# Retention and a softplus feed-forward net on one core: attention in groups of two steps, every fourth slot

## The chip, the cores and the metric

The kernel runs on one core of a Trainium2 chip. The metric is the device time of one execution, in microseconds (us). The engines are named as in the profile: PE is the matrix engine, PEld its loading of weights, DVE, ACT and POOL the vector, scalar and general engines, SP the queue that issues the transfers.

## The reference

Eight sequences of 576 tokens, eight heads of 64 features. Attention is a retention: scores decay with distance, there is no softmax. Its output, 4608 tokens by 512 features, goes through a two-layer net with a softplus between.

```python
def _attn_ref(q, k, v):                      # (8, 8, 576, 64) each
    scores = matmul(q, k.T) / sqrt(64)
    gamma = 1.0 - 2.0 ** (-5.0 - arange(8))  # one per head
    Dmat = where(rel >= 0, gamma ** rel, 0.0)  # rel = query position - key position
    return matmul(scores * Dmat, v)

def _moe_ref(x, w_in, w_out):                # x (4608, 512), w_in (512, 2048), w_out (2048, 512)
    h = x @ w_in
    g = maximum(h, 0.0) + log1p(exp(-abs(h)))
    return g @ w_out
```

## The kernel before

**The net.** The 4608 tokens are cut into 9 units of 512. A unit goes through 16 slots, one for each 128 of the 2048 hidden features, so there are 144 slots (`for i in range(NSLOT)`). A slot has these parts. On PE, `hidden_mm(i)` makes h for 128 features and 512 tokens from 12 products of 128x128 weights with 512 columns: 4 blocks of input features times 3 terms, since each 32-bit number is split into a high and a low part. ACT then takes the absolute value of h, the exponential and the logarithm (`logs`, L270 to L272); DVE adds max(h, 0) (`softplus`, L276, which reads h from PSUM); ACT rounds the result to the high part of g (L280), and DVE subtracts for the low part (`softplus_rest`, L284). Last on PE comes `output_mm(i - 1)`: the slot before's g times w_out, again 12 products, which add to four banks y over the 16 slots of the unit. So PE's order in each slot is hidden products of this slot, output products of the slot before. After a unit's last output products ACT and DVE copy two banks y each to SBUF (L304, L306) and SP sends them off.

**PSUM.** There are eight banks: four hold y, two hold h in turn (`ps_h`, two buffers, so that h of one slot can be written while h of the slot before is still read), and two hold one attention tile, `bank` (`ps_att`, one buffer of two banks).

**Attention.** The tokens are also cut into 36 chunks of 128, and heads into four pairs; a step is one chunk and two pairs (four heads), so there are 72 steps, two for each chunk. Nine steps are done in an opening ahead of the slots. After that each odd slot begins with one visit of PE to attention, for step m, 9 + (i - 1) / 2, until slot 127. A visit has four products of 64x64 blocks, each product 8 such matmuls (the profile has two records for each, 16 in all): the scores of step m (`scores`, L156), its sums of keys times values for the running state (`sums`, L169), and, for step m - 1, the masked scores times values (`values`, L220) and the state times queries (`cross`, the second loop of `values`, L231). Sequences begin at the start or in the middle of a chunk; some steps there have half of their sums or of their L231 matmuls only.

A 64x64 matmul takes one quadrant of PE's array: a row group (which 64 partitions of SBUF it reads) and a column group (which 64 partitions of PSUM it writes). In the text a quadrant is called a lane. `t` is the half of the chunk, `h` the head of the pair; the scores read row group h and write column group t, the other products read row group t and write column group h. All products of row group 0 go to the first of the two banks of `bank`, all of row group 1 to the second. The columns of a bank are divided into scores, sums and values.

**What follows a visit.** DVE multiplies the values by the decay (`values_out`, x, L241), ACT and POOL split x into its high and low parts for the net (L246, L247); DVE masks the scores (`scores_out`, a, L178) and adds up the state (`states_out`: u, sx and s, L201, L202, L210, or copies at a sequence's start); POOL copies half of sx and decays s (L194, L212). Then SP loads step m + 1 (`load_step`, one transfer of 576 KB into one of two buffers `rawp`), and POOL scales its values (L145). Results of step m's visit are used at the next visit, two slots later.

**What sets the order.** The order on each engine is the order in which the program writes its instructions; nothing is scheduled anew. Until about slot 15 the slots also turn the weights into their high and low parts as they arrive (`weight_...`), on ACT and DVE.

Of the kernel before, what the change touches and what calls it, by code (L numbers as in the profile page):

```python
# [33 lines left out]
KQ, RAW = 2 * C + 2 * QC, 6 * C + 2 * QC  # L34
SCOLS, TCOLS, VCOLS = slice(0, C), slice(C, 2 * C), slice(2 * C, 3 * C)
# [5 lines left out]
NOPEN = AHEAD + 2  # L41
FIRST_HALF = NF // 2
# [18 lines left out]
def retention_softplus_ffn(ctx: ExitStack, tc, first, others, consts, w, out):  # L61
# [56 lines left out]
    def load_step(m):  # L118

        if m == 0:  # L120
            at = 0
            for x in parts:
                nc.sync.dma_start(x, first[:, at:at + x.shape[1]])
                at += x.shape[1]
            kq, kv = parts[0][:, 0:KQ], parts[1][:, 0:4 * C]
# [23 lines left out]

    def scores(m, bank):  # L150
        if m >= NSTEP:
            return
        L = live[m]
        for s in range(2):
            for t, h in quads:
                nc.tensor.matmul(bank[rows[t], h, SCOLS][:, part[s]], L["k"][rows[h], s, part[t]],  # L156
                                 L["q"][rows[h], s, part[t]], start=True, stop=True, skip_group_check=True)
        L["bank"] = bank

    def sums(m):  # L160

        if m >= NSTEP:
            return
        L = live[m]
        start, follows = _chunk_kind(m // 2)
        for s in range(2):
            for t, h in quads:
                if follows if t else start != HC:
                    nc.tensor.matmul(L["bank"][rows[h], t, TCOLS][:, part[s]], L["kp"][rows[t], s, rows[h]],  # L169
                                     L["v"][rows[t], s, rows[h]], start=True, stop=True, skip_group_check=True)  # L170

    def scores_out(m):

        if m >= NSTEP:
# [4 lines left out]
                             L["bank"][:, :, SCOLS].rearrange("p h (s c) -> p h s c", s=2),  # L179
# [3 lines left out]
    def states_out(m):  # L183
# [6 lines left out]
        sum0, sum1 = (L["bank"][:, t, TCOLS].rearrange("p (s d) -> p s d", s=2) for t in range(2))  # L190
# [23 lines left out]

    def values(m, bank):

        L = live[m]
        for s in range(2):
            for t, h in quads:
                nc.tensor.matmul(bank[rows[h], t, VCOLS][:, part[s]], L["v"][rows[t], s, rows[h]],  # L220
                                 L["a"][rows[t], h, s], start=(s == 0), stop=L["states"][t] is None,
                                 skip_group_check=True)
        for s in range(2):
            for t, h in quads:
                if L["states"][t] is None:
                    continue
                if t == h:
                    lhs, rhs = L["states"][t], L["q"][rows[t], s, part[t]]
                else:
                    lhs, rhs = L["sx"], L["q"][rows[t], s, C:QC]  # L230
                nc.tensor.matmul(bank[rows[h], t, VCOLS][:, part[s]], lhs[rows[t], s], rhs, start=False, stop=True,  # L231
                                 skip_group_check=True)

    def values_out(m, bank, rest):

        live.pop(m)
# [5 lines left out]
                             bank[:, :, VCOLS].rearrange("p t (s c) -> p s t c", s=2),  # L242
# [11 lines left out]
    def hidden_mm(i, cols=slice(0, T)):  # L254
# [3 lines left out]
        h = ps_h.tile([P, T], F32, tag="h", name="h")[:, cols]  # L258
# [277 lines left out]
```

## Time and profile before

| | |
|---|---|
| time, median of 3 runs | 906.99 us (904.97 to 908.05) |
| time of the profiled execution | 907.14 us |
| its span, first to last instruction | 905.4 us |
| granted TensorE clock | 0.994 |
| busy in the span: PE, PEld | 889.3 us, 724.9 us |
| busy in the span: DVE, ACT, POOL | 366.4 us, 443.3 us, 144.9 us |
| transfers | 70.37 MB, mean 78 GB/s |

The span leaves 1.74 us of the profiled execution's time outside. A time in the trace counts from the start of the span. The row of a group gives the line of the kernel, the engine, the operation, the tile written and the tiles read, the shapes, the number of records, the busy time and the mean of one record, and behind the second bar the idle time ahead of it on its engine with what ended it. In the chain of waits each piece is a start, a length, and the engine, tile and line that the time is put down to; consecutive records of a line are merged. In the timeline a merged row gives the start, the time from the first record's start to the last one's end, and what was idle before.

### The profile page before, as it was taken

Reading aid. Unit: us, or ns where it says so; the run is one execution under the profiler, and the core shown is the slowest. Engines: PE = TensorE matmul, PEld = TensorE weight load, DVE = VectorE, ACT = ScalarE, POOL = GpSimd, SP = SyncE. Lnnn points to the kernel's source line nnn. Section 1 sums busy time; section 2 is a strip of 40 time slices with the busy share of each in tenths; the row PEclk is TensorE's granted clock in tenths of the full one; section 3 lists DMA queues with packets and bytes.
Section 4 is the critical chain, followed back from the end, with each engine's and each line's share of the span. In section 5 each row is a group of like instructions: output and inputs, shape, how many; then the busy total and the mean of one; then the engine's idle time right before and its main releaser. Section 6 shows DMA issues by size and latency. Waiting matters only on the chain.

```text
span 905.4 us, 18152 instructions
## 1 busy us (share of the span) xinstructions
PE 889.3 (98%) x7826; PEld 724.9 (80%) x7826; DVE 366.4 (40%) x742; ACT 443.3 (49%) x771; POOL 144.9 (16%) x269
## 2 busy tenths in 40 slices
PE   6899999999999999999999999999999999999998
PEld 5677778888888888888888888888888888888886
DVE  5788963333332343333333333323332432332222
ACT  5687764344444444444444444444444444445444
POOL 3312211111111111111111111111111111100000
PEclk9899999999999999999999999999999999999999
DMA  9565623111211131111211131113111121101001
GB/s 362 185 206 199 211 81 100 53 54 54 98 33 49 54 100 54 54 52 38 90 54 53 54 100 53 30 51 101 53 54 54 64 67 50 54 1 47 1 1 46
DMA packets 20527, 70.37 MB, mean 78 GB/s; under 512 B 2272, under 2 KB 2272, under 8 KB 20448
## 3 DMA queue, kind: packets, MB, share of 16 engines
q1 hardware_dynamic: 20448, 69.23, 22.9%
q8 instruction: 61, 1.00, 0.5%
q14 instruction: 18, 0.15, 0.0%
HBM read 59.78 MB, written 9.44 MB: 76 GB/s over the span
## 4 chain that ended last, share of the span: by engine, by line
PE 92%; DVE 4%; DMA 2%; ACT 1%; issue 1%; SPq 0%; DVEq 0%
PE h L262 43%; PE y L296 41%; PE bank L156 3%; PE bank L220 2%; PE bank L231 2%; PE bank L169 2%; DMA raw<-others 1%; DVE w L355 1%; DVE g L284 1%; DMA wst<-w 0%; DVE x L241 0%; DVE a L178 0%; ACT ab L272 0%; ACT ab L271 0%; ACT ab L270 0%
## 5 line engine op out<-in xcount | busy, mean ns | idle before, releaser
L262 PE MATMUL h<-xt,w 128*128 128x512 f32 (+1 forms) x1740 | 426.7, 395 | 0.0
L296 PE MATMUL y<-w,g 128*128 128x512 f32 x1728 | 415.8, 390 | 1.3 <-DVE g L284 1.3
L296 PEld LDWEIGHTS y<-w,g 128*128 128x128 f32 x1728 | 324.0, 188 | 70.7 <-DVE g L284 3.8
L262 PEld LDWEIGHTS h<-xt,w 128*128 128x128 f32 x1740 | 321.8, 189 | 69.1 <-ACT xt L246 0.6
L276 DVE SCALAR_TENSOR_TENSOR ab<-h,ab 128x512 f32<-128x512 f32 (+1 forms) x145 | 99.8, 688 | 427.2 <-ACT ab L272 427.2
L270 ACT ACTIVATE ab<-h 128x512 f32<-128x512 f32 (+1 forms) x145 | 86.3, 595 | 257.6 <-PE h L262 257.6
L280 ACT CAST g<-ab 128x512 fp32r<-128x512 f32 (+1 forms) x145 | 89.5, 617 | 102.5 <-DVE ab L276 101.3
L284 DVE TENSOR_TENSOR g<-ab,g 128x512 fp32r<-128x512 f32 (+1 forms) x145 | 101.3, 699 | 90.6 <-ACT g L280 89.2
L247 POOL TENSOR_TENSOR xt<-x,xt 128x256 fp32r<-128x256 f32 x71 | 54.6, 769 | 470.8 <-ACT xt L246 470.5
L271 ACT ACTIVATE ab<-ab 128x512 f32<-128x512 f32 (+1 forms) x145 | 91.2, 629 | 4.6
L272 ACT ACTIVATE ab<-ab 128x512 f32<-128x512 f32 (+1 forms) x145 | 91.2, 629 | 4.6
L246 ACT CAST xt<-x 128x256 fp32r<-128x256 f32 x72 | 29.2, 406 | 68.3 <-DVE x L241 68.3
L145 POOL TENSOR_TENSOR rawp<-rawp,consts_sb 128x256 f32<-128x256 f32 x61 | 39.9, 655 | 110.2 <-DMA rawp<-others 110.2
L156 PEld LDWEIGHTS bank<-rawp 64*64 64x64 f32 x976 | 19.8, 133 | 21.5 <-issue 21.5
L212 POOL TENSOR_TENSOR s<-s,consts_sb 128x128 f32<-128x128 f32 x55 | 23.9, 435 | 60.5 <-DVE s L210 49.3
L156 PE MATMUL bank<-rawp 64*64 64x64 f32 x976 | 28.2, 231 | 0.0
L350 ACT CAST w<-wst 128x512 fp32r<-128x512 f32 x32 | 21.2, 663 | 13.5 <-DVE wst L342 13.3
L220 PE MATMUL bank<-a,rawp 64*64 64x64 f32 x976 | 27.3, 220 | 0.0
L241 DVE TENSOR_TENSOR x<-bank,consts_sb 128x256 f32<-128x256 f32 x64 | 26.7, 418 | 0.0
L178 DVE TENSOR_TENSOR a<-bank,mask 128x256 f32<-128x256 f32 x63 | 26.2, 416 | 0.0
L231 PE MATMUL bank<-rawp,sx 64*64 64x64 f32 x440 | 25.2, 218 | 0.0
L169 PE MATMUL bank<-rawp 64*64 64x64 f32 x864 | 25.2, 218 | 0.0
(70 smaller groups left out, 411.2 us busy)
## 6 DMA issues: line engine op xcount, KB each, us to landing
rawp<-others SPq DMA_DIRECT2D x61, 576.0 KB, 4.0
wst<-w SPq DMA_DIRECT2D x32, 512.0 KB, 4.1
out<-osb SPq DMA_DIRECT2D x36, 256.0 KB, 2.4
raw<-others SPq DMA_DIRECT2D x10, 576.0 KB, 8.8
part<-first SPq DMA_DIRECT2D x1, 512.0 KB, 3.7
part<-first SPq DMA_DIRECT2D x1, 326.0 KB, 2.9
consts_sb<-consts SPq DMA_DIRECT2D x1, 262.0 KB, 5.8
```

What stands on the lines that cost most here:

```text
L156: nc.tensor.matmul(bank[rows[t], h, SCOLS][:, part[s]], L["k"][rows[h], s, part[t]], L["q"][rows[h], s, part[t]], start=True, stop=True, s ...
L169: nc.tensor.matmul(L["bank"][rows[h], t, TCOLS][:, part[s]], L["kp"][rows[t], s, rows[h]], L["v"][rows[t], s, rows[h]], start=True, stop=T ...
L220: nc.tensor.matmul(bank[rows[h], t, VCOLS][:, part[s]], L["v"][rows[t], s, rows[h]], L["a"][rows[t], h, s], start=(s == 0), stop=L["states ...
L247: rest.tensor_sub(lo, x, hi.bitcast(F32))
L262: nc.tensor.matmul(h, ws[p][:, a, kt * P:(kt + 1) * P], xt[:, b, kt, cols], start=(n == 0), stop=(n == 3 * NKT - 1))
L270: nc.scalar.activation(ab, h, AF.Abs)
L271: nc.scalar.activation(ab, ab, AF.Exp, scale=-1.0)
L272: nc.scalar.activation(ab, ab, AF.Ln, bias=1.0)
L276: nc.vector.scalar_tensor_tensor(ab, h, 0.0, ab, op0=ALU.max, op1=ALU.add)
L280: nc.scalar.copy(g[:, HI], ab)
L284: nc.vector.tensor_sub(g[:, LO], ab, g[:, HI].bitcast(F32))
L296: nc.tensor.matmul(y, g[:, a, at:at + P], ws[p][:, b, PIECE:], start=(p == 0 and n == 0), stop=(p == NF - 1 and n == 2))
```

## The change

From chunk 9 on, which is slot 19 (`by_chunks`), attention is visited in every fourth slot only (slots 19, 23 and so on to 127), and a visit does two steps, a whole chunk. In a visit of chunk ch the scores and sums are those of both steps of ch, the values and state products those of both steps of ch - 1 (of one step in slot 19, and no scores or sums in slot 127). Before slot 19 everything is as it was, except that the transfers of steps 11 and up are two for a step, k and its transposed copy in one of 256 KB, q and v in one of 320 KB.

The products are paired anew (`chunk_products`). Four phases follow one another; in each, matmuls of one product on row group 0 alternate with matmuls of another product on row group 1: sums (row group 0) with scores (1), scores (0) with values (1), values (0) with state products (1), state products (0) with sums (1). Each lane still gets the same number of matmuls. The place of the results changes: `bank` (two banks) has scores and values of two steps; the sums of both steps lie in a third bank, for both row groups. That third bank is the second bank of h, which therefore has one bank only from slot 19 on (the tags h0 and h1). The sums of row group 0 are written in the first phase and those of row group 1 in the last; between the two DVE copies one column of the first ones (`mark`), and the last phase's first matmul waits for that copy.

With one bank for h, `hidden_mm` of a slot waits until h of the slot before has been read. From slot 18 on DVE therefore makes r = max(h, 0) right after ACT's absolute value (`positive`), and `softplus` reads r from SBUF. From slot 18 on the subtraction for the low part of g (`softplus_rest`) is put off to the start of the next slot, behind the copy `mark` where that slot has a visit and behind the copies of y at a unit's end. Buffers for q and v of odd chunks are added, so that each load can be issued a visit ahead.

PE's order in one visit before (L156 scores, L169 sums, L220 values, L231 state products, then the hidden products of the slot):

```order
L296 MATMUL y_4605<-w_96,g 128x512 x3
L156 MATMUL bank<-rawp 64x64 [waits DMAHW4_49,PE_49]
L156 MATMUL bank<-rawp 64x64 x7
L169 MATMUL bank<-rawp 64x64 [waits Pool_49]
L169 MATMUL bank<-rawp 64x64 x7
L220 MATMUL bank<-a,rawp 64x64 x8
L231 MATMUL bank<-rawp,s 64x64
L231 MATMUL bank<-rawp,sx 64x64 x2
...
L262 MATMUL h<-xt_3655,w_98 128x512 x12
```

And in a visit of the change, a chunk in the middle of a sequence (L173 sums, L157 scores, L229 values, L241 state products; lines of the changed kernel), the first rows of the first phase and the first of the last:

```order
L352 MATMUL y_3799<-w_100,g 128x512 x3
L173 MATMUL sums<-qv,keys 64x64 [waits DMAHW3_49,DMAHW4_49,PE_49,Pool_49]
L157 MATMUL bank<-qv,keys 64x64 [waits PE_49]
...
L241 MATMUL bank<-qv,s 64x64
L173 MATMUL sums<-qv,keys 64x64 [waits DVE_49]
L241 MATMUL bank<-qv,sx 64x64
L173 MATMUL sums<-qv,keys 64x64
...
L312 MATMUL h<-xt_2942,w_102 128x512 x12
L352 MATMUL y_3796<-w_101,g 128x512 [waits DVE_49]
...
L312 MATMUL h<-xt_2942,w_994 128x512 [waits DVE_49]
```

The two kinds of matmul alternate one by one; one wait for DVE stands in the middle of the visit, ahead of the last phase, and one ahead of the hidden products of each slot without a visit, where there was none.

DVE's order around a visit before (L276 and L284 of the slot before, the visit's results, L276 and L284 of the visit's slot):

```order
L276 SCALAR_TENSOR_TENSOR ab<-h,ab 128x512 [waits Activation_49]
L284 TENSOR_TENSOR g<-ab,g 128x512 [waits PE_49,Activation_49]
L241 TENSOR_TENSOR x<-bank,consts_sb 128x256 [waits PE_49,Pool_49]
L178 TENSOR_TENSOR a<-bank,mask 128x256
L201 TENSOR_TENSOR u<-bank,s 128x128 [waits Pool_49]
L202 TENSOR_TENSOR sx<-bank,s 64x128
L210 TENSOR_TENSOR s<-bank,u 128x128 [waits DVE_49]
```

And in the change (L328 is r, L332 the softplus, L279 the copy `mark`, L340 the low part of g, L291 x, L190 a, L213, L214 and L222 the state, which come twice):

```order
L328 TENSOR_SCALAR r<-h 128x512 [waits Activation_49]
L332 SCALAR_TENSOR_TENSOR ab<-r,ab 128x512 [waits DVE_49,Activation_49]
L279 COPY mark<-sums 128x1 [waits PE_49]
L340 TENSOR_TENSOR g<-ab,g 128x512 [waits Activation_49]
L291 TENSOR_TENSOR x<-bank,consts_sb 128x256 [waits PE_49,Pool_49]
L291 TENSOR_TENSOR x<-bank,consts_sb 128x256 [waits Pool_49]
L190 TENSOR_TENSOR a<-bank,mask 128x256 x2
L213 TENSOR_TENSOR u<-sums,s 128x128 [waits PE_49,Pool_49]
L214 TENSOR_TENSOR sx<-sums,s 64x128
L222 TENSOR_TENSOR s<-sums,u 128x128 [waits DVE_49]
...
L328 TENSOR_SCALAR r<-h 128x512 [waits Activation_49]
```

The copy `mark` stands ahead of the low part of g, the ten results of a visit ahead of the next r, and r waits for ACT on its own, ahead of the softplus's wait.

The core of the diff:

```diff
             if m < NOPEN:
                 r = openp.tile([P, RAW], F32, name=f"raw{m}")
+                nc.sync.dma_start(r, others[m - 1])
+                keys, qv = r[:, 0:KEYS], r[:, KEYS:]
             else:
-                r = rawp.tile([P, RAW], F32, tag="rawp", name="rawp")
-            nc.sync.dma_start(r, others[m - 1])
-            kq, kv = r[:, 0:KQ], r[:, KQ:]
-        k = kq[:, 0:2 * C].rearrange("p (s c) -> p s c", s=2)
-        q = kq[:, 2 * C:].rearrange("p (s c) -> p s c", s=2)
-        kv = kv.rearrange("p (a s c) -> p a s c", a=2, s=2)
-        live[m] = dict(k=k, q=q, kp=kv[:, 0], v=kv[:, 1])
+                keys = rawp.tile([P, KEYS], F32, tag="keys", name="keys")
+                nc.sync.dma_start(keys, others[m - 1][:, 0:KEYS])
+                place = later["odd"] if m >= 2 * CHUNKS and m // 2 % 2 else rawp
+                qv = place.tile([P, RAW - KEYS], F32, tag="qv", name="qv")
+                nc.sync.dma_start(qv, others[m - 1][:, KEYS:])
+            k, kp, q, v = keys[:, 0:2 * C], keys[:, 2 * C:], qv[:, 0:2 * QC], qv[:, 2 * QC:]
+        live[m] = {n: x.rearrange("p (s c) -> p s c", s=2) for n, x in dict(k=k, q=q, kp=kp, v=v).items()}
...
+    def scores_mm(m, s, t, h):
+        L = live[m]
+        nc.tensor.matmul(L["S"][rows[t], h, part[s]], L["k"][rows[h], s, part[t]], L["q"][rows[h], s, part[t]],
+                         start=True, stop=True, skip_group_check=True)
     def scores(m, bank):
         if m >= NSTEP:
             return
-        L = live[m]
+        live[m]["S"] = bank[:, :, SCOLS]
         for s in range(2):
             for t, h in quads:
-                nc.tensor.matmul(bank[rows[t], h, SCOLS][:, part[s]], L["k"][rows[h], s, part[t]],
-                                 L["q"][rows[h], s, part[t]], start=True, stop=True, skip_group_check=True)
-        L["bank"] = bank
-
-    def sums(m):
-
-        if m >= NSTEP:
-            return
+                scores_mm(m, s, t, h)
+    def sums_mm(m, s, t, h):
         L = live[m]
         start, follows = _chunk_kind(m // 2)
+        if follows if t else start != HC:
+            nc.tensor.matmul(L["T"][rows[h], t, part[s]], L["kp"][rows[t], s, rows[h]], L["v"][rows[t], s, rows[h]],
+                             start=True, stop=True, skip_group_check=True)
+    def sums(m, bank):
+        if m >= NSTEP:
+            return
+        live[m]["T"] = bank[:, :, TCOLS]
         for s in range(2):
             for t, h in quads:
-                if follows if t else start != HC:
-                    nc.tensor.matmul(L["bank"][rows[h], t, TCOLS][:, part[s]], L["kp"][rows[t], s, rows[h]],
-                                     L["v"][rows[t], s, rows[h]], start=True, stop=True, skip_group_check=True)
+                sums_mm(m, s, t, h)
...
+    def values_mm(m, s, t, h, clear):
+        L = live[m]
+        nc.tensor.matmul(L["O"][rows[h], t, part[s]], L["v"][rows[t], s, rows[h]], L["a"][rows[t], h, s],
+                         start=clear, stop=L["states"][t] is None, skip_group_check=True)
+    def cross_mm(m, s, t, h):
+        L = live[m]
+        if L["states"][t] is None:
+            return
+        if t == h:
+            lhs, rhs = L["states"][t], L["q"][rows[t], s, part[t]]
+        else:
+            lhs, rhs = L["sx"], L["q"][rows[t], s, C:QC]
+        nc.tensor.matmul(L["O"][rows[h], t, part[s]], lhs[rows[t], s], rhs, start=False, stop=True,
+                         skip_group_check=True)
...
+    def chunk_products(steps, done):
+        bank = ps_att.tile([P, 2, T], F32, tag="bank", name="bank")
+        third = ps_h.tile([P, 2, 2 * C], F32, tag="h1", name="sums") if steps else None
+        for j, m in enumerate(steps):
+            live[m]["S"] = bank[:, :, j * C:(j + 1) * C]
+            live[m]["T"] = third[:, :, j * C:(j + 1) * C]
+        for m in done:
+            live[m]["O"] = bank[:, :, 2 * C + m % 2 * C:3 * C + m % 2 * C]
+        def together(*products):
+            for j in range(2):
+                for s in range(2):
+                    for o in range(2):
+                        for g, (f, which) in enumerate(products):
+                            if j < len(which):
+                                t, h = (o, g) if f is scores_mm else (g, o)
+                                clear = (j == s == 0,) if f is values_mm else ()
+                                f(which[j], s, t, h, *clear)
+        together((sums_mm, steps), (scores_mm, steps))
+        if steps and _chunk_kind(steps[0] // 2)[0] != HC:
+            mark = moe.tile([P, 1], F32, tag="mark", name="mark")
+            nc.vector.tensor_copy(mark, third[:, 0, 0:1])
+        together((scores_mm, steps), (values_mm, done))
+        together((values_mm, done), (cross_mm, done))
+        together((cross_mm, done), (sums_mm, steps))
...
-        h = ps_h.tile([P, T], F32, tag="h", name="h")[:, cols]
+        h = ps_h.tile([P, T], F32, tag=f"h{tag}", name="h")[:, cols]
...
+    def positive(h):
+        r = later["r"].tile([P, T], F32, tag="r", name="r")
+        nc.vector.tensor_scalar_max(r, h, 0.0)
+        return r
...
-    ps_h = ctx.enter_context(tc.tile_pool(name="ps_h", bufs=2, space=PSUM))
+    ps_h = ctx.enter_context(tc.tile_pool(name="ps_h", bufs=1, space=PSUM))
...
+    by_chunks = 2 * (2 * CHUNKS - AHEAD) + 1
+    rest = []
     for i in range(NSLOT):
         n = START_WEIGHTS + 2 * i
         m = AHEAD + (i - 1) // 2
-        step = i % 2 and m <= NSTEP
+        step = i % 2 and i < by_chunks
+        ch = CHUNKS + (i - by_chunks) // 4
+        chunk = i >= by_chunks and (i - by_chunks) % 4 == 0 and ch <= NCHUNK
+        if chunk:
+            done = [2 * ch - 2, 2 * ch - 1] if ch > CHUNKS else [2 * ch - 1]
+            steps = [2 * ch, 2 * ch + 1] if ch < NCHUNK else []
+            chunk_products(steps, done)
+        for f in rest:
+            f()
+        rest = []
         if step:
             bank = ps_att.tile([P, 2, T], F32, tag="bank", name="bank")
             scores(m, bank)
-            sums(m)
+            sums(m, bank)
...
-        h = hidden_mm(i)
+        h = hidden_mm(i, i % 2 if i < by_chunks else 0)
         if step and n >= NPIECE:
-            values_out(m - 1, bank, nc.gpsimd)()
+            values_out(m - 1, nc.gpsimd)()
             scores_out(m)
             states_out(m)
-            if m + 1 < NSTEP:
-                load_step(m + 1)
-            scale_values(m + 1)
+            for k in (m + 1,) if i < by_chunks - 2 else (m + 1, m + 2):
+                load_step(k)
+                scale_values(k)
+        if chunk:
+            for m in done:
+                values_out(m, nc.gpsimd)()
+            for m in steps:
+                scores_out(m)
+            for m in steps:
+                states_out(m)
+            for m in steps:
+                if m + 2 < NSTEP:
+                    load_step(m + 2)
+                    scale_values(m + 2)
         ab = logs(h)
+        if i >= by_chunks - 1:
+            h = positive(h)
         weight_dl(n - 1)
         softplus(h, ab)
...
-        softplus_rest(gs[i][0], ab)
+        if i < by_chunks - 1:
+            softplus_rest(gs[i][0], ab)
+        else:
+            rest.append(lambda g=gs[i][0], ab=ab: softplus_rest(g, ab))
...
-            later["osb"] = ctx.enter_context(tc.tile_pool(name="osb", bufs=4, side="right"))
+            for name, bufs in (("osb", 4), ("odd", 2), ("r", 1)):
+                later[name] = ctx.enter_context(tc.tile_pool(name=name + "2", bufs=bufs, side="right"))
...
-    hs = [hidden_mm(i, slice(n, n + T // 2)) for n in (0, T // 2)]
+    hs = [hidden_mm(i, n, slice(n * T // 2, (n + 1) * T // 2)) for n in range(2)]
```

More of the change, by code (lines that the diff above doesn't have):

```diff
@@ L41 @@
 NOPEN = AHEAD + 2
+CHUNKS = 9
 FIRST_HALF = NF // 2
@@ L189, in states_out @@
         before = states.get(m % 2) if start != 0 else None
-        sum0, sum1 = (L["bank"][:, t, TCOLS].rearrange("p (s d) -> p s d", s=2) for t in range(2))
+        sum0, sum1 = (L["T"][:, t].rearrange("p (s d) -> p s d", s=2) for t in range(2))
         sx = att.tile([P, 2, D], F32, tag="sx", name="sx")
@@ L215, in values @@
     def values(m, bank):
-        L = live[m]
+        live[m]["O"] = bank[:, :, VCOLS]
         for s in range(2):
             for t, h in quads:
-                nc.tensor.matmul(bank[rows[h], t, VCOLS][:, part[s]], L["v"][rows[t], s, rows[h]],
-                                 L["a"][rows[t], h, s], start=(s == 0), stop=L["states"][t] is None,
-                                 skip_group_check=True)
+                values_mm(m, s, t, h, s == 0)
         for s in range(2):
             for t, h in quads:
[L225 to L232, printed above, removed]
@@ L234, in values_out @@
-    def values_out(m, bank, rest):
-        live.pop(m)
+                cross_mm(m, s, t, h)
+    def chunk_products(steps, done):
[22 more added lines that the diff above has]
+        together((cross_mm, done), (sums_mm, steps))
@@ L237, in values_out @@
+    def values_out(m, rest):
+        L = live.pop(m)
         ch, pr = m // 2, 2 * (m % 2)
@@ L384, in retention_softplus_ffn @@
             scores(m, pair)
-            sums(m)
+            sums(m, pair)
         if m > 0:
@@ L389, in retention_softplus_ffn @@
             scores(m, pair)
-            sums(m)
-            values_out(m - 1, bank, nc.vector)()
+            sums(m, pair)
+            values_out(m - 1, nc.vector)()
         if m < AHEAD - 1:
@@ L424, in retention_softplus_ffn @@
             scores(m, bank)
-            sums(m)
+            sums(m, bank)
             values(m - 1, bank)
@@ L445, in retention_softplus_ffn @@
         if step and n < NPIECE:
-            parts_out = values_out(m - 1, bank, nc.gpsimd)
+            parts_out = values_out(m - 1, nc.gpsimd)
             scores_out(m)
@@ L503 @@
     kv = [x.transpose(0, 2, 3, 1, 4, 5) for x in (k, v)]
-    kq = by_partition(k_d, np.concatenate([q, crossed(q)], axis=5))
+    q = np.concatenate([q, crossed(q)], axis=5)
+    kq = by_partition(k_d, q)
+    others = by_partition(k_d, kv[0], q, kv[1])
     kv = by_partition(*kv)
@@ L521 @@
         "first": np.concatenate([kq[0], vsc, gchp, kv[0], decp], axis=1).astype(np.float32),
-        "others": np.concatenate([kq[1:], kv[1:]], axis=2),
+        "others": others[1:],
         "consts": np.concatenate([vsc, gchp, decp], axis=1).astype(np.float32),
```

16 lines of the change are left out of this document (9 added, 7 removed).

## The prediction

> **What bounds the kernel now.** I read the page's busy times and its chain of waits first, then the chain in one stretch of the middle, then the timeline there.
>
> ```profile
> span 905.4 us, 18152 instructions
> PE 889.3 (98%) x7826; PEld 724.9 (80%) x7826; DVE 366.4 (40%) x742; ACT 443.3 (49%) x771; POOL 144.9 (16%) x269
> PE 92%; DVE 4%; DMA 2%; ACT 1%; issue 1%; SPq 0%; DVEq 0%
> ```
>
> PE is busy for 98% of the span and carries 92% of the chain, no other engine is busy for half of it. So only what shortens PE's own work can gain, and what makes PE wait loses at once. The chain from 397.68 us, one visit of attention and what lies around it:
>
> ```profile
> 397.68 2.72 PE h L262 x12
> 400.40 2.72 PE y L296 x12
> 403.11 0.39 PE bank L156 x16
> 403.51 0.23 PE bank L169 x16
> 403.74 0.23 PE bank L220 x16
> 403.97 0.23 PE bank L231 x16
> 404.21 2.95 PE h L262 x12
> 407.16 2.72 PE y L296 x12
> 409.88 2.72 PE h L262 x12
> 412.60 2.72 PE y L296 x12
> 415.31 0.39 PE bank L156 x16
> ```
>
> PE never waits here for another engine. Twelve large matmuls take 2.72 us, a slot without a visit 5.44. From visit to visit it is 415.31 - 403.11 = 12.20 us, so a visit costs 12.20 - 2 x 5.44 = 1.32 us. Of that, 4 x 0.23 = 0.93 us (to the third digit 0.2325 each, from 403.04 to 403.97 and a quarter) are the four products. The rest, 0.39 us, is paid at the visit's two edges: 0.16 in the first product (0.39 in place of 0.23) and 0.23 in the hidden products behind it (2.95 in place of 2.72). In the timeline the first edge is PEld's idle time, which no other engine ends:
>
> ```profile
> 403.04 0.33 PEld L156 LDWEIGHTS bank<-rawp 64*64 64x64 f32 x16 [0.35 <-issue]
> ```
>
> Is the 0.39 us really a price per visit, and not a share of its work? The last visit, slot 127, has only two of the four products:
>
> ```profile
> 802.63 2.72 PE y L296 x12
> 805.35 0.39 PE bank L220 x16
> 805.75 0.23 PE bank L231 x16
> 805.98 2.95 PE h L262 x12
> ```
>
> Half the work, and the same 0.16 and 0.23 at the edges. The price is per visit.
>
> **The change, term by term.** Removed: visits. From slot 19 to slot 127 there are 55 before (odd slots) and 28 after. How much PE time they hold is read from one window and one group of it:
>
> ```profile
> 146.71:805.91 659.20, 659.20 (x5891) 537.93 (x5889) 229.66 (x481) 296.41 (x499) 106.19 (x203) 1.00 0.18 58
> L220 PE MATMUL bank<-a,rawp 64*64 64x64 f32 x880 | 24.6, 220 | 0.0
> ```
>
> 880 records of the values, 16 for each visit, are 55 visits. The window goes from the last large matmul before slot 19's visit to the first behind slot 127's and holds 108 slots: 659.20 - 108 x 5.44 = 71.7 us for the 55 visits, which agrees with 55 x 1.32 = 72.6 less the few that lack matmuls. PE is busy for all of it at full clock (1.00).
>
> Kept: the matmuls. A full visit of two steps has 8 products' worth, 8 x 0.2325 = 1.86 us if the lanes run as they do now, and with the edges 2.25 us against 2 x 1.32 = 2.64. 26 such visits are 58.5 us. Slot 19's has 6 products' worth and slot 127's 4; if phases where one row group has less still last as long as the fuller one, they take 2.0 and 1.8 us, if the lanes run ahead of each other 1.8 and 1.3. Sum 61.6 to 62.3 us, I take 62.0. So 71.7 - 62.0 = **9.7 us** are gained.
>
> Do the lanes keep their pace when two products alternate? Where steps lack half a product, the trace has such a mixture:
>
> ```profile
> 257.29 0.06 PE bank L169 x2
> 257.35 0.04 PE bank L220
> 257.39 0.06 PE bank L169 x2
> 257.45 0.01 PE bank L220
> ...
> 257.81 2.96 PE h L262 x12
> ```
>
> Sums (one row group only) and values (the other) run side by side here; from 256.89 to 257.81 that visit took 0.92 us against 1.10 for a full one (403.11 to 404.21), 0.18 us less; each lane had 12 records in place of 16, which at 0.2325 / 4 = 0.058 us a record are at most 0.23 us. Two products on two row groups do not disturb each other. Order makes no difference either: the scores (L156) change the row group with each matmul, as all products will, the sums (L169) with every second, and both take 0.23 us.
>
> Added, with an answer in other work:
>
> ```profile
> 402.39 0.69 DVE L276 SCALAR_TENSOR_TENSOR ab<-h,ab 128x512 f32<-128x512 f32 x1 [3.37 <-ACT ab L272]
> 403.77 0.69 DVE L284 TENSOR_TENSOR g<-ab,g 128x512 fp32r<-128x512 f32 x1 [0.68 <-ACT g L280]
> 404.38 0.42 DVE L241 TENSOR_TENSOR x<-bank,consts_sb 128x256 f32<-128x256 f32 x1
> ...
> 405.04 0.28 DVE L201 TENSOR_TENSOR u<-bank,s 128x128 f32<-128x128 f32 x1
> ...
> 405.67 0.29 DVE L210 TENSOR_TENSOR s<-bank,u 128x128 f32<-128x128 f32 x1
> ...
> 407.19 0.60 ACT L270 ACTIVATE ab<-h 128x512 f32<-128x512 f32 x1 [1.96 <-PE h L262]
> ```
>
> *r and the single bank for h.* In 125 slots, 18 to 142, r = max(h, 0) is made, in some 0.69 us (L276, which also reads h from PSUM; L306's copy from PSUM is near it). It waits for ACT's absolute value, which ends 0.60 us after its start at 407.19, so r runs from about 407.85 to 408.55; the next hidden products follow at 409.88 in the chain. Cover: about 1.2 us. In a visit's slot DVE first has ten results in place of five: two x and two a at steps of 0.33 us (two such steps from 404.38 to 405.04), six state results at 0.31 (two from 405.04 to 405.67): 3.2 us from 0.17 us behind the visit, so until about 407.6 on this scale, just before r could begin anyhow. Cost 0; without that cover, all that r is late beyond 1.2 us is PE's, in each slot.
>
> *The wait in the middle of a visit.* The last phase's sums wait for the copy `mark`, and behind them stand the rest of that phase and the hidden products. The first phase's records end some 0.47 + 0.2 us after the visit's start at 403.04; with 0.17 us to DVE (404.21 to 404.38) and at most 0.28 for the copy (L201's is 128 columns wide, this has one) it is done by 404.15. DVE is free from 403.08 on and the copy stands ahead of the low part of g. The last phase starts 3 x 0.465 = 1.40 us after the visit's start, at 404.44. Cover 0.3 us; cost 0, and at most the excess over that if DVE is late.
>
> *The low part of g put off* behind `mark`, or behind two copies of y at a unit's end. There:
>
> ```profile
> 424.63 2.88 PE L296 MATMUL y<-w,g 128*128 128x512 f32 x12
> ...
> 426.79 0.69 DVE L276 SCALAR_TENSOR_TENSOR ab<-h,ab 128x512 f32<-128x512 f32 x1 [3.37 <-ACT ab L272]
> ...
> 428.78 1.28 DVE L306 COPY osb<-y 128x512 f32<-128x512 f32 x2
> ```
>
> The copies would run from 427.5 to 428.8, the low part to 429.5; without the visit that stood there, the products that need it come 5.44 us after 424.63, at 430.07, their weights 0.2 earlier. Cover 0.35 us, cost 0, at most some 0.3 x 8.
>
> *Transfers and POOL.* Two for a step in place of one, four after a visit; SP has nothing else for three slots:
>
> ```profile
> rawp<-others SPq DMA_DIRECT2D x61, 576.0 KB, 4.0
> L145 POOL TENSOR_TENSOR rawp<-rawp,consts_sb 128x256 f32<-128x256 f32 x61 | 39.9, 655 | 110.2 <-DMA rawp<-others 110.2
> ```
>
> Two steps' loads end to end are 8 us, and 2 x 0.66 us of scaling; the next visit is 4 x 5.44 + 2.25 = 24 us later. At the first such visit they are issued 2 slots ahead, 12 us, which still holds. Cost 0, or up to 1 us in the stage where weights are loaded too, where each step's load is split.
>
> Sum: 905.4 - 9.7 = 895.7 us of span; with the 1.74 us outside, 897.4 us against the profiled 907.14. That execution lies 0.15 us over the median of 906.99, so the prediction for a median is the same **897.4 us** to within that. Its own range, from 1 us more gain to 2 or 3 us lost in covers that are only 0.3 us thick: 896 to 900.
>
> **The rivals.**
> *The new pairing makes the lanes faster.* If a weight load were hidden under the other row group's matmul where now it is not, a lane's 0.058 us per record would shrink; if to half, 26 x 0.93 = 24 us more, 873 us. For it: the row group changes with each matmul in all four products and not in one. Against it: that one, L156, takes 0.23 us like the others. 3 in 100. [...]
>
> *Slower: the single bank for h.* Place: the first hidden matmul of each slot. If r came only after ACT's logarithm, like the softplus now, it would end where L276 ends (403.08, 0.03 us before PE went on at 403.11), and with a handover of 0.17 us, as from PE to DVE above, PE would lose 0.14 us in each of 125 slots: 17.5 us, so 915 us. It decides from 9.7 / 125 = 0.08 us per slot. For it: h had two banks, and PE now waits for DVE in every slot. Against it: in the order r has a wait of its own ahead of the softplus's, so it needs the absolute value alone; cover 1.2 us. 6 in 100. [...]
>
> *Slower: lanes that hinder each other,* say sums and scores of one phase in turn: 26 x 1.86 = 48 us more, 946 us; from 0.070 us per record on ((2.64 - 0.39) / 32). Against it the mixture at 257 us. 3 in 100.
>
> *No gain.* The edges grow with the visit, or the wait for `mark` takes the 0.39 us back (DVE 0.7 us later than reckoned): 907 us. Against it slot 127's visit and DVE's idle time. 7 in 100.
>
> *Half the gain,* from covers that are too thin in some of the visits, 902 us: 6 in 100. [...]
>
> **How the numbers follow.** The forecast has 75 in 100. A measurement of this kernel tells about 0.3%, 2.7 us, from no change. Faster: forecast, faster lanes and half the gain, 75 + 3 + 6 = 84; same: 7; slower: 6 + 3 = 9. The range is the forecast's, widened to half the gain at the upper end (902) and to 895 below, where the lanes run ahead of each other in visits that lack matmuls.
>
> **What would show it.** Right: 28 visits from slot 19 on, chain pieces of 0.39 and then 0.23 per 16 records, 1.86 + 0.39 us in all, the hidden products behind them 2.95 and all others 2.72; visits 24.0 us apart (12.20 x 2 - 0.39); r over 1 us before the next hidden products. Wrong: idle time of PE ahead of L312 ended by DVE r (single bank), ahead of L173 ended by `mark`, or ahead of L352 after a unit's end; phases of over 0.47 us (lanes).

## The result, and the profile after

The changed kernel takes 899.87 us (median of four runs, 898.95 to 901.04) against 907.05 us (four runs, 904.97 to 908.05): a ratio of 0.9925, with an interval of 0.9903 to 0.9946. It is faster, by 7.2 us or 0.8% where the prediction had 9.7 us; the time lies inside the range of 895 to 902. The profiled execution took 900.48 us, with a span of 898.8 us and a granted clock of 0.994.

The page of the changed kernel: span, busy times, shares of the chain of waits.

```profile
span 898.8 us, 18538 instructions
PE 885.1 (98%) x7826; PEld 727.4 (81%) x7826; DVE 461.2 (51%) x891; ACT 441.2 (49%) x771; POOL 146.4 (16%) x269
PE 94%; DVE 3%; ACT 1%; issue 1%; DMA 1%; POOL 0%; SPq 0%; POOLq 0%
```

PE is still the bound: the same 7826 matmuls in 4.2 us less busy time. DVE has 95 us more to do (366.4 to 461.2), and that shows nowhere in the chain's shares. One visit in the chain of the changed kernel (L173 sums, L312 hidden products, L352 output products):

```profile
381.83 2.72 PE h L312 x12
384.55 2.75 PE y L352 x12
387.29 0.20 PE sums L173
...
388.85 0.47 PE sums L173 x16
389.32 2.95 PE h L312 x12
392.27 2.75 PE y L352 x12
395.01 2.72 PE h L312 x12
...
408.67 2.75 PE y L352 x12
411.41 0.20 PE sums L173
```

The visit runs from 387.29 to 389.32, 2.03 us, and its hidden products take 0.23 us more than the others (2.95 in place of 2.72): 2.26 us together, where the prediction had 2.25. From visit to visit it is 411.41 - 387.29 = 24.12 us, 0.11 us more than 4 x 5.44 + 2.25 = 24.01. Those 0.11 us are nearly all in the four groups of output products, which now read 2.75 us in place of 2.72; the visit itself has 0.01 of them. The same window as before the change, from the last large matmul before slot 19's visit to the first behind slot 127's, with all instructions and then with the output products alone:

```profile
146.03:798.68 652.65, 652.65 (x5890) 538.45 (x5888) 312.50 (x613) 294.31 (x498) 106.18 (x201) 1.00 0.18 58
...
146.03:798.68 652.65, 314.63 (x1298) 243.40 (x1296) 1.00 0.18 58
```

The output products alone in the kernel before (start and end, length, PE's busy time, PEld's, clock, share of the DMA engines, GB/s):

```profile
146.71:805.91 659.20, 311.70 (x1298) 243.40 (x1296) 1.00 0.18 58
```

PE is busy for the whole window in both, at full clock (1.00). The output products, the same 1298 records, take 314.63 - 311.70 = 2.93 us more, 0.027 us in each of 108 slots. So the 28 visits hold 652.65 - 108 x 5.44 - 2.93 = 62.2 us: the predicted 62.0, from 71.7.

Is it the visits that disturb the output products? The group of all output products on the page, before and after:

```profile
L296 PE MATMUL y<-w,g 128*128 128x512 f32 x1728 | 415.8, 390 | 1.3 <-DVE g L284 1.3
```

```profile
L352 PE MATMUL y<-w,g 128*128 128x512 f32 x1728 | 419.6, 392 | 0.9 <-DVE g L340 0.9
```

The whole execution has 3.8 us more of it, not only the window's 2.93. And in the chain of the changed kernel the longer group is there in a slot near the start, when no visit is of the new kind and neither r nor `mark` exists, as it is in slots behind the last visit:

```profile
62.55 2.75 PE y L352 x12
...
839.97 2.75 PE y L352 x12
```

To the third digit, over stretches without a visit, it is 2.7475 us in place of 2.720, in all 144 slots: 144 x 0.0275 = 3.96 us. The hidden products between them keep 2.72.

The account of the span, 905.4 - 898.8 = 6.6 us, by its three parts: the window 659.20 - 652.65 = 6.55 us shorter (9.5 by the visits, 2.9 given back); ahead of it 0.68 us shorter (146.71 to 146.03) although 18 slots of output products cost 0.5 there; behind it 0.63 us longer (905.4 - 805.91 = 99.49 to 898.8 - 798.68 = 100.12), of which the output products are 0.5. The 1.2 us that the first part has won lie in the opening: slot 1's output products, the first of the program, start between 35.8 us (a_w480) and 40.3 us (a_w448) in the traces of this case. Counted from their start to the end of the span, which leaves the opening out, it is 905.4 - 38.0 = 867.4 us before and 898.8 - 37.4 = 861.4 after, 6.0 us less.

### The profile page after: what moved, and what is told of

It reads as the page before. It is cut to its first block, busy times and chain, and to the rows that moved or that the text cites. A ratio compares the mean times of both kernels' runs of the same rounds, so it can differ in the third digit from the quotient of the medians.

```text
span 898.8 us, 18538 instructions
## 1 busy us (share of the span) xinstructions
PE 885.1 (98%) x7826; PEld 727.4 (81%) x7826; DVE 461.2 (51%) x891; ACT 441.2 (49%) x771; POOL 146.4 (16%) x269
## 4 chain that ended last, share of the span: by engine, by line
PE 94%; DVE 3%; ACT 1%; issue 1%; DMA 1%; POOL 0%; SPq 0%; POOLq 0%
PE h L312 43%; PE y L352 43%; PE sums L173 2%; PE bank L157 2%; PE bank L229 2%; PE bank L241 2%; DMA raw<-others 1%; DVE w L411 0%; DVE g L340 0%; DVE a L190 0%; DVE x L291 0%; ACT ab L321 0%; ACT ab L322 0%; ACT ab L320 0%; PE pair L157 0%
## 5 line engine op out<-in xcount | busy, mean ns | idle before, releaser
L312 PE MATMUL h<-xt,w 128*128 128x512 f32 (+1 forms) x1740 | 422.0, 392 | 0.0
L352 PE MATMUL y<-w,g 128*128 128x512 f32 x1728 | 419.6, 392 | 0.9 <-DVE g L340 0.9
L352 PEld LDWEIGHTS y<-w,g 128*128 128x128 f32 x1728 | 324.0, 188 | 73.2 <-DVE g L340 3.4
L312 PEld LDWEIGHTS h<-xt,w 128*128 128x128 f32 x1740 | 323.3, 188 | 68.9 <-ACT xt L296 0.3
L328 DVE TENSOR_SCALAR r<-h 128x512 f32<-128x512 f32 x125 | 86.5, 692 | 214.5 <-ACT ab L320 214.5
L340 DVE TENSOR_TENSOR g<-ab,g 128x512 fp32r<-128x512 f32 (+1 forms) x145 | 102.5, 707 | 69.3 <-ACT g L336 68.0
L332 DVE SCALAR_TENSOR_TENSOR ab<-r,ab 128x512 f32<-128x512 f32 x125 | 89.1, 713 | 79.6 <-ACT ab L322 79.6
L150 POOL TENSOR_TENSOR qv<-qv,consts_sb 128x256 f32<-128x256 f32 x61 | 42.3, 693 | 54.6 <-DMA qv<-others 54.4
L157 PE MATMUL bank<-qv,keys 64*64 64x64 f32 x976 | 34.0, 222 | 0.0
L291 DVE TENSOR_TENSOR x<-bank,consts_sb 128x256 f32<-128x256 f32 x64 | 24.6, 419 | 17.9 <-PE sums L173 12.4
L173 PEld LDWEIGHTS sums<-qv,keys 64*64 64x64 f32 x768 | 26.5, 134 | 8.6 <-issue 8.6
L229 PE MATMUL bank<-a,qv 64*64 64x64 f32 x976 | 32.9, 218 | 0.0
L157 PEld LDWEIGHTS bank<-qv,keys 64*64 64x64 f32 x976 | 29.4, 134 | 3.6 <-issue 3.6
L173 PE MATMUL sums<-qv,keys 64*64 64x64 f32 x768 | 32.0, 221 | 0.0
L229 PEld LDWEIGHTS bank<-a,qv 64*64 64x64 f32 x976 | 29.9, 135 | 0.4 <-issue 0.4
```

The source lines that it names most:

```text
L157: nc.tensor.matmul(L["S"][rows[t], h, part[s]], L["k"][rows[h], s, part[t]], L["q"][rows[h], s, part[t]], start=True, stop=True, skip_grou ...
L173: nc.tensor.matmul(L["T"][rows[h], t, part[s]], L["kp"][rows[t], s, rows[h]], L["v"][rows[t], s, rows[h]], start=True, stop=True, skip_gro ...
L229: nc.tensor.matmul(L["O"][rows[h], t, part[s]], L["v"][rows[t], s, rows[h]], L["a"][rows[t], h, s], start=clear, stop=L["states"][t] is No ...
L312: nc.tensor.matmul(h, ws[p][:, a, kt * P:(kt + 1) * P], xt[:, b, kt, cols], start=(n == 0), stop=(n == 3 * NKT - 1))
L328: nc.vector.tensor_scalar_max(r, h, 0.0)
L332: nc.vector.scalar_tensor_tensor(ab, h, 0.0, ab, op0=ALU.max, op1=ALU.add)
```

## The experiments

**Where the question lay.** The visit's price had come out as worked out; what was open was why products that the change does not touch lost 2.3 ns per matmul. Three theories. *Extra work*: DVE's additional 95 us, or r in SBUF, disturbs PE's reading. *Address*: the tile w (weights of the net) lies at another place in SBUF. *Distance*: what counts is how far w (the operand that streams through PE in the output products) lies from g (the one loaded as weights). The change moves w: `mark`, two buffers of 32 bytes per partition, is allocated in the pool `moe`, between g and w. In the built program g starts at byte 31168 of a partition in both kernels, w at 81344 before and at 81408 now, so the distance went from 50176, a multiple of 256, to 50240, that is 64 more. (These are the starts of the first w and of the first of g's two buffers; the other w, the other buffer and the blocks within a tile all lie multiples of 512 bytes from them, so one figure modulo 256 holds for all output products.) xt lies behind the same 64 bytes as w, so the hidden products (w loaded, xt streamed) keep their distance, 32768 for the first buffer of xt.

**The changed kernel again.**

> The changed kernel once more, on the chip of the next three, so that they have it beside them. Both theories: 0.99 of the kernel before (0.9903 to 0.9946 so far), some 900 us; visits of 2.25 us, output products of 2.75 us a slot where the kernel before has 2.72.

It took 901.0 us, ratio 0.9938 (0.9916 to 0.9960) to 905.46 us before.

**64 bytes more in each kernel.** An unused tile ahead of xt and w:

```diff
     mask = const.tile([P, HC], F32, name="mask")
+    pad = rawp.tile([P, 16], F32, name="pad", bufs=1)
+    nc.gpsimd.memset(pad, 0.0)
```

In the changed kernel (distance 50304, 128 over a multiple of 256):

> The changed kernel with 64 unused bytes per partition ahead of the input tiles xt and the weights w, so that w lies 50304 bytes behind g, a multiple of 128, as it was a multiple of 128 (50176) in the kernel before; in the changed kernel it is 50240, which is 64 over such a multiple. Theory 'place in SBUF' (the output products, which load g as weights and stream w, lose 2.3 ns each where the two lie 64 bytes apart modulo 128): output products back to 2.72 us a slot, 144 x 0.027 = 3.9 us less than the changed kernel, some 896 us, ratio to before 0.988. Theory 'work beside it' (DVE's 86 us of r, or ACT and DVE reading PSUM while PE writes it, slow the output products): 2.75 us a slot and 900 us as they are.

In the kernel before (distance 50240, 64 over):

> The kernel before with the same 64 unused bytes, so that w lies 50240 bytes behind g as in the changed kernel, and nothing else changed. Theory 'place in SBUF': the output products go from 2.72 to 2.75 us in each slot, 3.9 us in all, 911 us, ratio 1.004. Theory 'work beside it': no difference, 907 us.

The kernel before became slower with it: 910.57 us, ratio 1.0049 (1.0032 to 1.0066), 5.1 us more; 4.0 of them are the output products' 144 x 0.0275, the rest is within the interval's width. Its groups and its chain:

```profile
L298 PE MATMUL y<-w,g 128*128 128x512 f32 x1728 | 419.5, 392 | 1.2 <-DVE g L286 1.2
```

```profile
604.97 2.72 PE h L264 x12
607.69 2.75 PE y L298 x12
```

Here is the changed kernel's loss without any of its work: 64 bytes alone make 2.75 of 2.72. The theory of extra work falls. In the changed kernel the pad cost too, where I had expected it to give the time back (a distance modulo 128): 910.95 us, ratio 1.0047 (1.0030 to 1.0064), with

```profile
L354 PE MATMUL y<-w,g 128*128 128x512 f32 x1728 | 426.6, 395 | 0.6
```

```profile
602.40 2.76 PE h L314 x12
605.15 2.80 PE y L354 x12
```

The output products take 2.80 us, and the hidden ones beside them 2.76 although their own distance is the old one. Behind a visit, though, the hidden products take the 2.95 us that they took before; only those behind output products are longer:

```profile
395.65 2.95 PE h L314 x12
398.61 2.80 PE y L354 x12
401.40 2.76 PE h L314 x12
```

So the loss comes with the output products ahead of them, and the hidden products' own distance stays free. Whatever the period is, it is not 128.

**Address or distance.** 64 bytes ahead of all tiles but the constants and the mask, so that g and w both move and their distance stays that of the changed kernel; then the same with the pad as well. The tile `lead` is the one added:

```diff
     mask = const.tile([P, HC], F32, name="mask")
+    lead = const.tile([P, 16], F32, name="lead")
+    nc.gpsimd.memset(lead, 0.0)
```

> The changed kernel with the 64 unused bytes ahead of g too: g and w both move by 64, their distance stays 50240. If the distance of g and w decides: output products 2.75 us a slot, as in the changed kernel. If w's own address modulo 128 decides (64 here, as in the kernel before): 2.72 us. Theory 'work beside it': 2.75 us.

> The changed kernel with 64 unused bytes ahead of g and 64 more ahead of xt and w: g's address is 0 and w's 0 modulo 128, their distance 50304, a multiple of 128. If the distance decides: output products 2.72 us a slot. If w's own address modulo 128 decides (0, as in the changed kernel): 2.75 us.

The first took 901.33 us in one execution, its output products as in the changed kernel; the second 912.72 us, 2.80 and 2.76 us. The groups of the first and of the second:

```profile
L354 PE MATMUL y<-w,g 128*128 128x512 f32 x1728 | 419.6, 392 | 1.1 <-DVE g L342 1.1
```

```profile
L356 PE MATMUL y<-w,g 128*128 128x512 f32 x1728 | 426.6, 396 | 0.9 <-DVE g L344 0.4
```

With `lead` alone w starts at byte 81472, exactly where it starts with `pad` alone; the output products take 419.6 us with the one and 426.6 with the other. So it is not w's address. At one distance and two addresses the sums are the same (419.6 and 419.6; 426.6 and 426.6). It is the distance from something that lies ahead of the pad.

One rival is left. Other tiles of the pool `moe`, `ab` among them, keep their distance from g in all these edits, and ACT and DVE read and write them: is it w against g, or w against what other engines do? The starts of single matmuls settle that. In the changed kernel the twelve intervals of an output group are 229, 232, 226 ns, four times over (the last one 227), against 226 or 227 each in the kernel before. The last group of the program, from 891.91, has the same three in turn. There r and `mark` are not in use any more, and the other engines finish g by 892.98 and then only copy y to SBUF. So the loss goes by the product in a block of three, not by what runs beside it. It is the distance of w from g.

**Other distances.** The changed kernel with pads of 32, 192, 448 and 480 bytes (columns of `pad`: 8, 48, 112, 120):

> The changed kernel with 32 unused bytes ahead of xt and w: the distance of g and w is 50272, 96 modulo 128 and 32 modulo 64. If 64-byte places matter (a read of 64 bytes that straddles two of them), something between 2.72 and 2.80 us for the output products, and the hidden products, whose w and xt both start off a multiple of 64 now, may get slower too; if only the distance modulo 128 near zero is fast, 2.75 us.

> The changed kernel with 192 unused bytes ahead of xt and w: distance 50432, which is 256 modulo 512. Output products so far by distance modulo 512: 2.72 us at 0, 2.75 at 64, 2.80 at 96 and 128. If the period is 256: 2.72 us. If it is 512 and the loss lasts to the middle: 2.80 us or more.

> The changed kernel with 448 unused bytes ahead of xt and w: distance of g and w 50688, a multiple of 512 like 50176, but no multiple of 1024; all addresses other than in any kernel so far. If the distance modulo 512 decides (steps between the blocks of g and of w are multiples of 512 bytes, so no larger period can hold for all matmuls alike): 2.72 us a slot, 896.5 us. If only the old addresses are fast: 2.75 us or more, 900 us or more.

> The changed kernel with 480 unused bytes ahead of xt and w: distance 50720, 32 modulo 512. If the loss grows with the distance: between 2.72 and 2.75 us. If it goes by whole steps of 64 bytes, with all off them at the full price (96 cost more than 64): 2.80 us.

And the change with `mark` in the pool of r, which lies beyond the weights, so that all tiles of the net are back in their old places. This is the change without its shift:

```diff
-            mark = moe.tile([P, 1], F32, tag="mark", name="mark")
+            mark = later["r"].tile([P, 1], F32, tag="mark", name="mark")
```

> The changed kernel with the copy's target mark, 64 bytes per partition between g and the weights w with its two buffers, put in the pool of r, beyond the weights. All tiles up to the last weights then lie as in the kernel before, g and w 50176 bytes apart. Theory 'distance of g and w': output products back to 2.72 us a slot, 144 x 0.027 = 3.9 us less than the changed kernel, some 896.5 us, ratio to before 0.988 to 0.989. If something else in the changed kernel slows the output products: 2.75 us, 900 us.

All kernels by the distance of g and w, the twelve output products of a slot, and the time (the kernel before: the median of the result above; otherwise one execution where no ratio stands):

| kernel | distance | over a multiple of 256 | output products, us | time, us; ratio (interval) |
|---|---|---|---|---|
| before | 50176 | 0 | 2.720 | 907.05 |
| the change, `mark` elsewhere (a_mark) | 50176 | 0 | 2.720 | 897.05; 0.9904 (0.9887 to 0.9921) |
| the change + 192 (a_w192) | 50432 | 0 | 2.720 | 897.43 |
| the change + 448 (a_w448) | 50688 | 0 | 2.720 | 896.18; 0.9889 (0.9869 to 0.9909) |
| the change + 480 (a_w480) | 50720 | 32 | 2.79 | 906.2 |
| the change | 50240 | 64 | 2.7475 | 899.87; 0.9925 (0.9903 to 0.9946) |
| the change, all moved (a_all64) | 50240 | 64 | 2.7475 | 901.33 |
| before + 64 (b_w64) | 50240 | 64 | 2.7475 | 910.57; 1.0049 (1.0032 to 1.0066) |
| the change + 32 (a_w32) | 50272 | 96 | 2.80 | 911.31 |
| the change + 64 (a_w64) | 50304 | 128 | 2.80 | 910.95; 1.0047 (1.0030 to 1.0064) |
| both pads (a_all64_w64) | 50304 | 128 | 2.80 | 912.72 |

Distances of 0 and of 256 over a multiple of 512 (a_w448, a_w192) are both free, 32 over is not: 256 bytes is the smallest period that fits all of them, if it is a period; between 128 and 256 over nothing was run. Up to 128 the price does not grow evenly; 64 is cheaper than 32 and than 128. So neither a price that grows with the distance fits (2.72 to 2.75 us were expected at 32 over) nor one on distances off a multiple of 64 bytes alone (128 is such a multiple and costs 2.80). The whole group of output products takes 415.8 and 415.7 us of PE with pads of 192 and 448 bytes, as before the change. With 192 bytes:

```profile
L354 PE MATMUL y<-w,g 128*128 128x512 f32 x1728 | 415.8, 390 | 1.2 <-DVE g L342 1.2
```

And with 480 bytes:

```profile
L354 PE MATMUL y<-w,g 128*128 128x512 f32 x1728 | 425.8, 395 | 0.8
```

The change in the old places: its page, its window (the same stretch as above), and its chain around one visit.

```profile
span 895.4 us, 18538 instructions
...
L352 PE MATMUL y<-w,g 128*128 128x512 f32 x1728 | 415.8, 390 | 1.0 <-DVE g L340 1.0
```

```profile
146.36:795.80 649.44, 649.44 (x5889) 538.33 (x5889) 311.78 (x612) 294.19 (x498) 104.66 (x201) 1.00 0.18 58
```

```profile
602.25 0.20 PE sums L173
...
604.27 2.95 PE h L312 x12
607.22 2.72 PE y L352 x12
609.94 2.72 PE h L312 x12
```

The window is 659.20 - 649.44 = 9.76 us shorter than before the change, 649.44 - 108 x 5.44 = 61.9 us of visits; the span is 895.4 us. This version and those with 448 and 192 bytes of pad are the fastest kernels of the study. The ratios' intervals of the first two overlap a little with that of the change, and the four executions with 448 bytes range from 895.39 to 900.04 us, so the times alone would not part them well; the pace of the output products in each trace does. So does the time from slot 1's first output product to the end: 867.4 us before, 861.4 for the change, 857.9 for a_mark, 858.0 and 858.1 with 448 and 192 bytes. That is 9.3 to 9.5 us gained in the old distance and 6.0 with the shift.

**The price of a visit, and the pairing.** Two edits of the kernel before. In the first the visits stay as many and as they are, but the products are paired as in the change, in four phases (`together` with `scores_mm` and the others of the change, for one step; there is no `mark`):

```diff
             bank = ps_att.tile([P, 2, T], F32, tag="bank", name="bank")
-            scores(m, bank)
-            sums(m)
-            values(m - 1, bank)
+            paired(m, bank)
...
+        together(sums_mm, scores_mm)
+        together(scores_mm, values_mm)
+        together(values_mm, cross_mm)
+        together(cross_mm, sums_mm)
```

> The kernel before with the new pairing alone, one step a visit in every second slot from slot 1 on, all products in the two banks as before. Theory of the prediction (the lanes' pace of 0.058 us a record is what counts, pairing is free): a visit stays at 1.32 us, 907 us, ratio 1.00. Rival (a weight load hides under the other row group's matmul): less than 1.32 us, at the least 0.39 + 0.47, so down to 880 us. Rival (lanes hinder each other): up to 2.25 us a visit, 960 us.

It took 906.43 us, ratio 1.0002 (0.9988 to 1.0016) to 906.61 us: no difference. Its chain from one visit to the next (L245 sums):

```profile
608.92 0.20 PE bank L245
...
610.01 2.95 PE h L308 x12
...
621.12 0.20 PE bank L245
```

From the hidden products behind a visit to the next visit it is 11.11 us, as before (415.31 - 404.21 = 11.10), and with the visit 621.12 - 608.92 = 12.20 us again. What the change gains comes from the number of visits, not from the pairing.

In the second edit the state products are taken out of `values` and put behind the hidden products of the slot, a visit of their own: 57 visits more with not one matmul more.

```diff
+    def cross(m, bank):
+        L = live[m]
         for s in range(2):
...
         h = hidden_mm(i)
         if step and n >= NPIECE:
+            cross(m - 1, bank)
             values_out(m - 1, bank, nc.gpsimd)()
```

> The kernel before with each visit from slot 15 on cut in two: scores, sums and values at the start of the slot, the state products behind the slot's hidden products. 57 more visits, the same matmuls. Theory of the prediction (0.39 us a visit whatever it holds): 57 x 0.39 = 22 us more, 929 us, ratio 1.024. Rival (the 0.39 us is a share of the work, or of the wait for results): 907 us, or up to 5 us more where results come later.

It took 929.45 us, ratio 1.0251 (1.0223 to 1.0278), 22.8 us more, or 0.40 us for each added visit. The chain (L235 state products):

```profile
601.54 0.39 PE bank L156 x16
...
602.39 2.95 PE h L266 x12
605.34 0.39 PE bank L235 x16
605.73 2.95 PE y L300 x12
608.68 2.72 PE h L266 x12
...
614.12 0.39 PE bank L156 x16
```

Both edges are paid a second time: the state products' 0.23 became 0.39, and the output products behind them took 2.95 in place of 2.72. The period grew from 12.20 to 614.12 - 601.54 = 12.58 us. So each change to 64x64 blocks and back costs 0.39 us; what PE does in that time the trace does not show.

## Why the prediction was right, and where it was not

**The price per visit, 0.39 us whatever it holds: right.** The visits of the changed kernel hold 62.2 us, in the version with the old places 61.9, where 62.0 were worked out. A full visit costs 2.26 us. b_split shows the price by itself.

**Lanes that keep their pace with two products in turn: right.** The last phase takes 0.47 us in the chain for 16 records of sums and as many of state products, eight in each lane (4 x 0.465 = 1.86 us a visit was the sum), and b_paired, with the new pairing alone, neither gains nor loses. The prediction had no direct reading of this: its 0.23 us for L156 is the 0.39 of the chain less the edge. That slot 127's visit begins with another product (L220), which takes 0.39 there and 0.23 elsewhere, speaks for it; b_paired shows it. The rivals of faster lanes (873 us) and of lanes that hinder each other (946 us) fall with it.

**The single bank for h, `mark`, the low part of g: right, all at no cost.** DVE around the visit at 387.29 in the timeline of the changed kernel (L328 is r, L279 `mark`, L340 the low part of g):

```profile
387.97 0.16 DVE L279 COPY mark<-sums 128x1 f32<-128x1 f32 x1 [0.73 <-PE sums L173]
388.05 0.68 DVE L340 TENSOR_TENSOR g<-ab,g 128x512 fp32r<-128x512 f32 x1
...
391.81 0.29 DVE L222 TENSOR_TENSOR s<-sums,u 128x128 f32<-128x128 f32 x1
392.94 0.69 DVE L328 TENSOR_SCALAR r<-h 128x512 f32<-128x512 f32 x1 [0.83 <-ACT ab L320]
```

`mark` is there at 388.13, and the first of the last phase's sums starts at 388.68 by the timeline: the cover is some 0.5 us, 0.3 were reckoned. The ten results end at 392.10, 0.83 us before ACT's absolute value releases r; r ends at 393.63 and the next hidden products follow at 395.01, 1.4 us later, 1.2 reckoned. Among PE's waits there is none for r or `mark`, and the one for g is smaller than before (1.3 us in 6 times):

```profile
PE y L352 <- DVE g L340: 0.9, 5, 0.2
```

So the rival of the slow single bank (915 us) falls too. That the change needs the wait for `mark`, and r only behind the absolute value, was not shown: no run of it is without them.

**What failed: a term that the sum did not have.** The prediction counted the matmuls as "kept", with all other large products at 2.72 us, and gave no price to where tiles come to lie in SBUF. The new tile `mark` cost nothing as a wait, and as 64 bytes 144 x 0.0275 = 3.96 us, or 3.8 by PE's busy time: it moved w against g, and each of the 144 groups of output products took 0.0275 us more. That is the difference to within the spread of the executions: by the spans of the profiled ones 895.4 us for a_mark, 898.8 for the change, 895.7 predicted; by the medians 897.05 and 899.87 to 901.0, with 897.4 predicted. Expected 9.7 us, measured with the shift 7.2 and without it 8.5 (905.56 - 897.05) and, with 448 bytes of pad, 9.4 (905.56 - 896.18). That the time stayed inside the range was luck as far as this term goes: the upper end was there for covers that are too thin, and these held. The term could have been much larger: at 128 bytes over the period it takes 2.80 us for the output products, 2.76 for the hidden ones behind them, and the changed kernel is slower than the one before (ratio 1.0047), with every other step of the prediction right.

**Transfers and POOL: no cost seen.** The stage ahead of the window became shorter, not longer, and POOL's busy time in the window is the same to 0.1 us (106.19 and 106.18).

**What stays open.** Which part of the chip loses the 2.3 to 6.7 ns per matmul (0.0275 and 0.08 us for twelve) is not shown. Weights are loaded while matmuls run: PE is busy for 885.1 us and PEld for 727.4 of the change's 898.8, so both are busy together for at least 885.1 + 727.4 - 898.8 = 713.7 us. That the readings of the two tiles collide at some distances is a guess of mine, which no run shows. The records of the output products' weight loads have the same mean (188 ns) at 0, 64 and 128 over. All kernels with a distance of 0 over have g in its old place, so a free distance with the loaded tile elsewhere was seen only in the hidden products, whose w and xt moved together by 64 bytes in the change and stayed at 2.72 us.

## What to carry to other kernels

Where PE is the bound and changes between 128x128 and 64x64 work, count the changes: each cost 0.39 us here, whatever stood between them, so the same matmuls in half as many visits gained half of that price; the pairing of row groups by itself gained nothing. Where many large matmuls with new weights each run back to back, write down the byte addresses of the loaded and of the streamed tile before and after an edit, small tiles too, and keep their distance a multiple of 256 bytes, as in the free cases here, or put new small tiles behind them. When products that an edit does not touch change their pace everywhere by the same few nanoseconds, look for what moved in memory before looking at what was added in work.

## What the runs showed of the hardware that was not expected

The interval of 128x512 matmuls with a new weight load each depends on the distance in SBUF of the loaded and the streamed tile: 2.720 us for twelve at a multiple of 256 bytes, 2.7475 at 64 over, 2.79 at 32 over, 2.80 at 96 and 128 over, up to 2.9% of these products. For the changed kernel the whole range is 896.18 to 912.72 us, more than the change itself gained. Where the output products are slowed to 2.80 the hidden products behind them, whose own tiles keep their distance, take 2.76 (a_w64) or 2.77 (a_w32); at 2.79 (a_w480, 32 over) they take 2.73. Between the kernel before and the same kernel with 64 unused bytes, PE's busy time in the output products differs by 3.7 us (415.8 and 419.5).
